# Dense block in fp32: rows normalised and turned from the tiles in which they were summed, one block later

## The chip, the cores and the metric

The kernel runs on one core of a Trainium2 chip. The metric is the device time of one launch in microseconds (us); less is better. Engines are named as the profile names them: PE (TensorE, matrix products), DVE (VectorE), ACT (ScalarE), POOL (GpSimd) and SP (SyncE, which here only issues DMAs).

## The reference

Two layers, each an attention block with 32 heads and then a dense block with a squared relu, all in fp32, on 2048 rows of 640 columns (the width F of the dense block is 1536). The normalisations have no weights.

```python
def _A_ref(x, wqkv, wo):                       # attention, 32 heads of 20
    q, k, v = split_heads(x @ wqkv)
    p = _softmax(einsum("bhqd,bhkd->bhqk", q, k) * (Dh ** -0.5))
    return merge_heads(einsum("bhqk,bhkd->bhqd", p, v)) @ wo
def _B_ref(x, w1, b1, w2, b2):                 # dense
    h = jnp.einsum("bsd,df->bsf", x, w1) + b1
    r = jnp.where(h > zero, h, zero)
    return jnp.einsum("bsf,fd->bsd", r * r, w2) + b2
for _ in range(2):
    x = x + _A_ref(_layernorm(x, axis=-1), A_wqkv, A_wo)
    x = x + _B_ref(_layernorm(x, axis=-1), B_w1, B_b1, B_w2, B_b2)
```

## The kernel before

Every fp32 operand of a product is split into a high and a low part, and three products of parts make one (`THREE`). The 2048 rows go in four blocks (`qb` 0 to 3) of 512, a block in four row tiles of 128 x 640. PSUM has eight banks, taken in turn.

A layer's dense block begins with the output projection, `add_heads(qb)`: for each row tile two chains of 15 matmuls (L361), half a row tile each, and a VectorE addition (L1355) that adds them to the tile of x; the finished tile is written to memory (`x_mid`, shown as `d_x<-x`). Then comes `mlp(fh, qb)`, for each half `fh` of the width F and each block: six "up" chains of 15 matmuls (L361) with relu and square on ScalarE (L1456, L1457, tiles `r`) and splits on VectorE (`upper` makes `ha`; `left_operands` makes three `hs` in seven instructions, L1438 to L1443 and L325), and then seven "low" products (L1482) whose banks VectorE adds to the rows (L1501; L1503 adds the bias). Half 0 leaves its sums in `d_half`, half 1 writes the next layer's input `x_e` (or the output).

An up chain needs the rows normalised and turned, tiles `xnT`, five of 128 x 512 for a block. Two generators make them, each step of which is run at a numbered place between the chains:

- `turn_out(d, xs)`: for each of four row tiles the statistics (L312, L313; POOL makes the reciprocal deviation at L315, L316), the normalisation in place (L320), a transpose of 32 x 32 squares into a tile `y` (L1389), and four stores of `y` into a buffer in memory, `d_t`, in pieces of 128 bytes.
- `turn_in(d, get)`: five loads xnT<-d_t, and for each a copy on ScalarE (L1405) and a subtraction on VectorE (L1406) that split it in two.

In the projection the places are the `side()` calls behind each half row (24 for the blocks behind the first); in an mlp they are one before it (-1), one behind each up chain, one behind the six, and one behind each low product. In half 1 the second use of a block's `xnT` comes from a copy in memory, `d_xn`.

Where the rows come from: block 0 is turned from the tiles in which `add_heads` summed it (`kept`). Blocks 1, 2 and 3 are read back from `x_mid` (`x<-d_x`), two tiles ahead: block 1 during the third and fourth block of the projection, block 2 in mlp(0,0), block 3 in mlp(0,1). In the first layer's half 1 the rows of block qb - 1 of the next layer's input are read back from `x_e` in mlp(1, qb). Block 3 of that input stays in tiles (`rows_3`) and is turned by PE (L476, in `turns`) at the hand-over, behind matmuls of the next layer's q, k, v (L399); `second()` yields the price by which those transposes are placed.

Each engine runs its instructions in the order written. All DMAs named here go through SP's queue in order, each waiting for the one eight places ahead of it; a tile of a pool is free for its next user when the last reader of the old contents is done, for `y` its stores. Row tiles, `y` and `r` share a pool of NX = 11 tiles of 2560 bytes a partition; xnT, hs, ha, weights and more share NSLOT = 42 tiles of 4096 bytes. An mlp also reads its own four rows (`row_tile(d_half if fh else x_mid, ...)`).

## Time and profile before

| | |
|---|---|
| median of 3 runs | 3516.32 us (3511.18 to 3517.25) |
| profiled execution | 3514.18 us, of which the span shown is 3512.4 us |
| granted PE clock, mean | 0.992 |
| busy, share of the span | PE 98%, DVE 81%, ACT 77%, POOL 23% |
| DMA | 533.20 MB, mean 152 GB/s; 179764 of 405510 packets under 512 bytes |
| dense block of layer 1 | 1342.5 to 1769.1 us of the span |
| dense block of layer 2 | 3095.4 to 3508.9 us |

All times in the profile count from the start of the span. "Waited for" names the last releaser of an instruction. PEclk is the granted clock of PE, 1.00 at full speed.

### The profile page before, as it was taken

What the parts mean: (1) busy time and instruction counts of PE and PEld (TensorE: products, weight loads), DVE (VectorE), ACT (ScalarE), POOL (GpSimd) and SP (SyncE); (2) the same over time, 40 slices, a digit from 0 to 9 for tenths busy, and PEclk for the clock granted to TensorE, in tenths of its full rate; (3) what the DMA queues carried; (4) which work ended last, traced back from release to release, by engine and by line L of the source; (5) the groups of instructions that cost most, each with busy time, mean ns of one, the idle gap of its engine ahead of it and who ended that gap; (6) DMA issues with size and microseconds to landing.
All of it is one profiled execution on the core that took longest, in us unless ns stands there. A gap on an engine that the chain in (4) does not pass through costs nothing.

```text
span 3512.4 us, 70196 instructions
## 1 busy us (share of the span) xinstructions
PE 3446.9 (98%) x26202; PEld 2158.6 (61%) x26202; DVE 2850.4 (81%) x5410; ACT 2705.2 (77%) x4362; POOL 800.5 (23%) x963
## 2 busy tenths in 40 slices
PE   9999999999999999899999999999999999998999
PEld 7897444444444447788889964444444444477898
DVE  8888999999999982656768889999999999726555
ACT  3778999999999992243337789999999999922433
POOL 6531445522112111100044201221221122111000
PEclk9999999999999999999999999999999999998999
DMA  9865555422211148957687652222232111488653
GB/s 311 280 239 170 182 159 180 149 74 77 61 51 46 43 121 256 282 209 253 175 280 264 204 161 80 69 77 66 68 83 58 52 43 43 129 264 265 213 224 109
DMA packets 405510, 533.20 MB, mean 152 GB/s; under 512 B 179764, under 2 KB 227380, under 8 KB 405168
## 3 DMA queue, kind: packets, MB, share of 16 engines
q1 hardware_dynamic: 404352, 526.35, 47.7%
q8 instruction: 206, 3.38, 0.4%
q10 hardware_dynamic: 816, 2.36, 0.2%
q14 instruction: 136, 1.11, 0.1%
HBM read 316.59 MB, written 211.98 MB: 150 GB/s over the span
## 4 chain that ended last, share of the span: by engine, by line
PE 90%; DVE 4%; DMA 3%; SPq 1%; ACT 1%; issue 1%; POOL 0%; DVEq 0%; POOLq 0%
PE banks L690 28%; PE banks L549 19%; PE banks L676 14%; PE banks L399 11%; PE banks L361 9%; PE banks L1482 7%; DMA x<-d_x 1%; SPq L76 1%; DVE bst L312 1%; DMA w<-d_w 1%; DVE x L320 0%; DVE y L1389 0%; ACT hs L324 0%; PE banks L1288 0%; DMA d_t<-y 0%
## 5 line engine op out<-in xcount | busy, mean ns | idle before, releaser
L561 DVE TENSOR_REDUCE mx<-banks 128x1 f32<-128x512 f32 x2096 | 1429.9, 686 | 136.9 <-PE banks L549 36.6
L549 PE MATMUL banks<-k,q 60*128 60x512 f32 (+1 forms) x4488 | 1310.3, 370 | 1.9 <-DVE v L445 1.9
L549 PEld LDWEIGHTS banks<-k,q 60*128 60x128 f32 x4488 | 714.7, 184 | 831.2 <-DVE mx L596 725.3
L684 ACT ACTIVATE e<-banks 128x512 f32<-128x512 f32 x1988 | 1194.1, 601 | 15.0 <-PE banks L676 2.2
L690 PE MATMUL banks<-e,vg 128*32 128x512 f32 x8192 | 1092.7, 605 | 1.5 <-ACT e L1295 1.5
L676 PE MATMUL banks<-q,k 62*128 62x512 f32 x3968 | 1074.3, 421 | 0.6 <-DVE mx L617 0.6
L686 ACT ACTIVATE e<-banks 128x1024 f32<-128x1024 f32 x990 | 1007.0, 1017 | 0.0
L596 DVE TENSOR_REDUCE mx<-banks 128x2 f32<-128x512 f32 x928 | 633.4, 682 | 3.3 <-PE banks L549 3.3
L676 PEld LDWEIGHTS banks<-q,k 62*128 62x128 f32 x3968 | 579.4, 184 | 53.8 <-ACT e L684 51.9
L617 DVE CUSTOM_DVE_ANT_0 rl<-banks,rl 128x512 f32<-128x512 f32 x536 | 350.2, 689 | 78.0 <-PE banks L549 57.2
L609 ACT ACTIVATE rl<-banks 128x512 f32<-128x512 f32 x538 | 295.7, 596 | 100.9 <-PE banks L549 80.2
L399 PE MATMUL banks<-xnT,wqk 64*128 64x512 f32 x2400 | 372.3, 393 | 0.9 <-DVE x L1501 0.6
L361 PE MATMUL banks<-xnT,w 128*128 128x512 f32 x1440 | 334.7, 393 | 11.0 <-DVE xnT L1406 8.1
L690 PEld LDWEIGHTS banks<-e,vg 128*32 128x32 f32 x8192 | 161.2, 108 | 260.7 <-issue 256.7
L399 PEld LDWEIGHTS banks<-xnT,wqk 64*128 64x128 f32 x2400 | 299.4, 186 | 25.6 <-issue 2.0
L361 PEld LDWEIGHTS banks<-xnT,w 128*128 128x128 f32 x1440 | 271.9, 190 | 69.6 <-DVE xnT L1406 10.1
L1482 PE MATMUL banks<-w,hs 128*128 128x320 f32 x1728 | 275.5, 319 | 20.4 <-DVE x L1501 13.5
L1482 PEld LDWEIGHTS banks<-w,hs 128*128 128x128 f32 x1728 | 266.2, 196 | 26.3 <-DVE x L1501 15.9
L1456 ACT ACTIVATE r<-banks,b_t 128x512 f32<-128x512 f32 x96 | 65.9, 687 | 261.1 <-PE banks L361 220.5
L339 POOL CAST mr<-nt 128x32 fp32r<-128x32 f32 x64 | 13.5, 212 | 1081.7 <-DVE nt L643 1081.7
L734 POOL TENSOR_TENSOR few<-few,minus_t 128x16 f32<-128x16 f32 x62 | 179.9, 2902 | 198.7 <-DMA few<-d_s 198.4
L399 PE MATMUL banks<-wv,xnT 64*128 64x320 f32 x1920 | 208.6, 307 | 0.8 <-ACT mark_t L401 0.8
(104 smaller groups left out, 2659.2 us busy)
## 6 DMA issues: line engine op xcount, KB each, us to landing
q<-d_qk SPq DMA_DIRECT2D x240, 240.0 KB
d_qk<-ev SPq DMA_DIRECT2D x80, 512.0 KB
k<-d_qk SPq DMA_DIRECT2D x152, 240.0 KB
w<-d_w SPq DMA_DIRECT2D x56, 480.0 KB
x<-d_x SPq DMA_DIRECT2D x84, 320.0 KB
d_qk<-ev SPq DMA_DIRECT2D x80, 256.0 KB
d_xn<-xnT SPq DMA_DIRECT2D x40, 512.0 KB
xnT<-d_xn SPq DMA_DIRECT2D x40, 512.0 KB
```

The costliest lines, as they stand in the source:

```text
L361: nc.tensor.matmul(dst, a, b, start=(n == 0), stop=(n == last))
L399: m = nc.tensor.matmul(ch["dst"][:, :width], *pair, start=first, stop=last)
L549: return nc.tensor.matmul(dst, q_t[t][b : b + 60, p, sub * P : (sub + 1) * P], k_t[t // NQB, c][b : b + 60, p, keys], start=True, stop=True,)
L561: nc.vector.tensor_reduce(maxima(t)[:, 2 * par + p, sub, c : c + 1], dst, axis=AX.X, op=ALU.max)
L596: r = nc.vector.tensor_reduce(maxima(t)[:, p : p + 3 : 2, sub, c if not half else column(t, p, sub)], bank.rearrange("q (r k) -> q r k", r=2),
L609: nc.scalar.activation(res, dst, AF.Relu)
L617: nc.vector.tensor_tensor_reduce(out=r, in0=dst, in1=r, scale=1.0, scalar=LEAST, op0=ALU.add, op1=ALU.max, accum_out=maxima(t)[:, 2 * par ...
L676: nc.tensor.matmul(dst, k_t[t // NQB, kt // 4][b : b + 62, p, (kt % 4) * P : (kt % 4 + 1) * P], q_t[t][b : b + 62, p, :], start=True, stop ...
L684: nc.scalar.activation(es[h], dst, AF.Exp, scale=SCALE)
L686: nc.scalar.activation(es[pair], banks[:, 1:3, :], AF.Exp, scale=SCALE)
L690: nc.tensor.matmul(acc[32 * h : 32 * h + 32, :], v_t[t // NQB, kt // 8][:, kt % 8, 32 * h : 32 * h + 32], es[h], start=(kt == 0), stop=(kt ...
L1482: nc.tensor.matmul(dst[:, :HALF], t[:, hx, c : c + P], w_2.piece(j, p, hw), start=start and p == 0 and (hx, hw) == THREE[0], stop=stop and ...
```

## The change

Every row tile that the projection sums is kept and turned during the block behind it: block 0 during qb = 1, block 1 during qb = 2, block 2 during qb = 3 and block 3 in mlp(0,0). In layer 1's half 1, the four row tiles that mlp(1, qb) finishes are kept (`rows`) and turned in mlp(1, qb + 1), their first statistics at place 18 of the mlp in which they were summed. No row is read back for turning, and `turn_out` loses its reads: 36 DMAs of 320 KB leave SP's queue (24 in layer 1, 12 in layer 2). By the order, all other counts stay (DVE 5412 instructions, ACT 4376, POOL 968, PE 22106).

`turn_in` of block 0 runs its steps at places 10, 14, 15, 17, 19, 21 of the projection (8, 12, 13, 16, 18, 20 before). The buffers `d_t` of the blocks are four in place of two in half 0. Rows 0 and 1 of the last block of layer 1 are normalised between its last low products, and `second()` yields 5.0 in place of 0.65. NX goes from 11 to 12, NSLOT from 42 to 41.

```diff
@@ -32,8 +32,8 @@
 LEAST = -3.0e38
 SCALE = DH ** -0.5
 NBLK = NG * NQB
-NSLOT = 42
-NX = 11
+NSLOT = 41
+NX = 12
 
 
 @with_exitstack
@@ -1355,17 +1355,11 @@
                 nc.vector.tensor_add(x[:, c], dst[:, :HALF], x[:, c])
                 side()
             dma(nc.sync, x_mid[(qb * 4 + i) * P : (qb * 4 + i + 1) * P, :], x)
-            if qb == 0:
-                kept.append(x)
+            kept.append(x)
+            x = None
 
     def turn_out(d, xs):
 
-        if callable(xs):
-            read, xs = xs, []
-            xs.extend(read(i) for i in range(2))
-        else:
-            read = None
-        yield
         y = None
 
         def store(i):
@@ -1387,8 +1381,7 @@
             normalise(nc.vector, xs[i], mvs[i])
             y = xtile("y")
             nc.vector.transpose(y, xs[i])
-            if read and i < 2:
-                xs.append(read(i + 2))
+            xs[i] = None
             yield
         store(3)
         xs.clear()
@@ -1416,7 +1409,7 @@
         nc.vector.tensor_scalar(y, x, mv[:, 0:1], mv[:, 1:2], op0=ALU.subtract, op1=ALU.mult)
         return y
 
-    def mlp(fh, qb, xnt, x_mid, x_dst, side, last):
+    def mlp(fh, qb, xnt, x_mid, x_dst, side, last, rows):
 
         xs, ops = [], {}
         w = QB // 2
@@ -1508,7 +1501,11 @@
                     dma(nc.sync, (x_dst if fh else d_half)[r0 : r0 + P, :], x)
                     if final and not last:
                         rows_3.append((x, stats(x) if j == 4 else None))
+                    elif fh and not last:
+                        rows.append(x)
                     xs[i] = None
+                if final and not last and (j, u) in ((5, 1), (6, 0)):
+                    rows_3[1 - u] = to_normal(*rows_3[1 - u])
                 x = None
                 side()
             if j == 0:
@@ -1522,12 +1519,10 @@
                 if not fh:
                     for n in (2 * j, 2 * j + 1):
                         w_2.load(1, n)
-        for i, (x, mv) in enumerate(rows_3[:]):
-            if i == 3:
-                rows_3[i] = x, stats(x)
-            else:
-                rows_3[i] = to_normal(x, mv or stats(x))
-        x = None
+        if final and not last:
+            for i in (2, 3):
+                rows_3[i] = rows_3[i][0], stats(rows_3[i][0])
+            rows_3[2] = to_normal(*rows_3[2])
 
     def layer(first, x_a, x_m, x_e, front_0, ahead):
         xs = []
@@ -1552,34 +1547,29 @@
         def rows_of(src, tb):
             return lambda i: row_tile(src, tb * 4 + i)
 
-        xnt, rows = [], []
-        plan = [[] for _ in range(24)]
-        outs = [turn_out(d_t[0], rows_of(x_m, 2))]
+        xnt = []
         loads = [
             [lambda s=s: w_1.load(s) for s in range(8)] + [lambda s=s: w_2.load(0, s) for s in range(3)],
             [lambda s=s: w_2.load(0, s) for s in range(3, 8)],
             [lambda s=s: w_2.load(0, s) for s in range(8, 12)],
             [],
         ]
-
+        plan = [[] for _ in range(24)]
+        in_0 = turn_in(d_t[0], lambda: xnt)
+        for i in (10, 14, 15, 17, 19, 21):
+            plan[i].append(lambda: next(in_0))
         for qb in range(NQB):
             if qb + 2 == NQB:
                 xnt.extend(new_rows())
+            rows = []
             add_heads(qb, x_a, x_m, xs, side, rows)
+            if qb + 1 < NQB:
+                gen = turn_out(d_t[qb], rows)
+                for i in (0, 1, 3, 5, 6, 7):
+                    plan[8 * qb + i].append(lambda gen=gen: next(gen))
             if qb == 0:
-                out_0 = turn_out(d_t[0], rows)
-                in_0 = turn_in(d_t[0], lambda: xnt)
-                out_1 = turn_out(d_t[1], rows_of(x_m, 1))
-                for gen, at in (
-                    (out_0, range(7)), (out_1, (13, 14, 15, 17, 19, 20)),
-                    (in_0, (8, 12, 13, 16, 18, 20)), (outs[0], (20,)),
-                ):
-                    for i in at:
-                        plan[i].append(lambda gen=gen: next(gen))
                 steps.extend([None] * (24 - len(steps)))
                 steps[:] = [(lambda n=n, f=f: [f and f()] + [g() for g in plan[n]]) for n, f in enumerate(steps)]
-            if qb == 1:
-                next(out_1)
             for f in loads[qb]:
                 f()
             if qb + 1 == NQB:
@@ -1587,6 +1577,8 @@
         w_o.drop()
         for s in range(12, w_2.n):
             w_2.load(0, s)
+        outs = [(turn_out(d_t[3], rows), (-1, -1, 0, 2, 4, 5))]
+        rows = None
         for fh, qb in ((fh, qb) for fh in range(2) for qb in range(NQB)):
             new = []
             plan = [[] for _ in range(22)]
@@ -1609,22 +1601,22 @@
                     dma(nc.sync, new[k], d_xn[qb, k])
 
             if not fh and qb + 1 < NQB:
-                put(turn_in(d_t[(qb + 1) % 2], to(new)), 6, 13, 14, 15, 16, 17)
+                put(turn_in(d_t[qb + 1], to(new)), 6, 13, 14, 15, 16, 17)
                 plan[20].append(lambda: [dma(nc.sync, d_xn[qb + 1, k], new[k]) for k in range(KD)])
             elif (fh, qb) != (1, NQB - 1):
                 plan[7].append(lambda: again((qb + 1) % NQB))
-            if not fh and qb + 2 < NQB:
-                put(outs.pop(0), -1, -1, 0, 2, 4, 5)
-            if not fh and qb + 3 < NQB:
-                outs.append(turn_out(d_t[(qb + 1) % 2], rows_of(x_m, qb + 3)))
-                put(outs[0], 17)
+            if outs:
+                put(*outs[0][:1], *outs.pop()[1])
+            rows = []
+            if ahead and fh and qb + 1 < NQB:
+                gen = turn_out(d_t[2 + qb], rows)
+                put(gen, 18)
+                outs.append((gen, (-1, 0, 2, 4, 5)))
             if (fh, qb) == (0, 0):
                 plan[4].append(lambda x=list(xnt): [dma(nc.sync, d_xn[0, k], x[k]) for k in range(KD)] and x.clear())
             if not fh and qb + 1 == NQB:
                 for n in range(7):
                     plan[(0, 0, 2, 4, 4, 4, 5)[n] + 1].append(lambda n=n: w_1.load(8 + n))
-            if ahead and fh and qb:
-                put(turn_out(d_t[1 + qb], rows_of(x_e, qb - 1)), -1, 0, 0, 2, 4, 6, 7)
             if ahead and fh and qb + 2 >= NQB:
                 for tb, at in enumerate((13, 6, 11)):
                     if (tb == 0) == (qb + 2 == NQB):
@@ -1636,7 +1628,8 @@
                     plan[11 + n].append(lambda n=n: w_qk.load(n))
             steps.extend((lambda p=p: [f() for f in p]) for p in plan)
             side()
-            mlp(fh, qb, xnt, x_m, x_e, side, not ahead)
+            mlp(fh, qb, xnt, x_m, x_e, side, not ahead, rows)
+            rows = None
             xnt = new
             all_steps()
         steps.clear()
@@ -1646,7 +1639,7 @@
 
 
         rows_3[3] = to_normal(*rows_3[3])
-        yield 0.65, turns(3, rows_3, ps_q, (1, 3))
+        yield 5.0, turns(3, rows_3, ps_q, (1, 3))
 
     def constants():
 
```

Three places as the order of instructions shows them, before and then after. Tiles carry a running number; lines of the changed kernel are six lower at the transpose (L1383 is L1389 of before) and seven lower behind it (L1494 is L1501).

SP's queue, layer 1, end of the projection and start of mlp(0,0). `d_x_111` is `x_mid`, `d_t_106` to `d_t_109` the buffers, `w` a weight tile. Before:

```order
698 L76 DMA d_t_107<-y_16189 32x20x32 x4
699 L76 DMA x_16214<-d_x_111 128x640
700 L76 DMA x_16216<-d_x_111 128x640
701 L76 DMA d_x_111<-x_15984 128x640
702 L76 DMA d_x_111<-x_16030 128x640
703 L76 DMA w_16268<-d_w_97 128x960
704 L76 DMA w_16270<-d_w_97 128x960
705 L76 DMA x_16289<-d_x_111 128x640
706 L76 DMA d_t_106<-y_16287 32x20x32 x4
707 L76 DMA x_16326<-d_x_111 128x640
708 L76 DMA x_16360<-d_x_111 128x640
709 L76 DMA x_16382<-d_x_111 128x640
```

After:

```order
694 L76 DMA d_t_108<-y_16167 32x20x32 x4
695 L76 DMA d_x_111<-x_15957 128x640
696 L76 DMA d_t_108<-y_16216 32x20x32 x4
697 L76 DMA d_x_111<-x_16011 128x640
698 L76 DMA d_t_108<-y_16265 32x20x32 x4
699 L76 DMA d_t_108<-y_16289 32x20x32 x4
700 L76 DMA d_x_111<-x_16060 128x640
701 L76 DMA w_16312<-d_w_97 128x960
702 L76 DMA w_16314<-d_w_97 128x960
703 L76 DMA d_t_109<-y_16331 32x20x32 x4
704 L76 DMA x_16400<-d_x_111 128x640
705 L76 DMA x_16422<-d_x_111 128x640
```

Of before, blocks 1 (`d_t_107`) and 2 (`d_t_106`) are being stored there, with reads `x<-d_x` between; two of these (16360, 16382) are mlp(0,0)'s own rows and stay. After, blocks 2 (`d_t_108`) and 3 (`d_t_109`) are being stored at this place, a block further on.

DVE in mlp(1,1) of layer 1, behind the split of the last `ha`, up to the first addition of a low product. In front of the rows of before stand, behind that split, the statistics L312 and L313 of the row 18210. Before:

```order
2101 L320 TENSOR_SCALAR x_18138<-x_18138,mv_18201 128x640
2102 L1389 STREAM_TRANSPOSE y_18281<-x_18138 128x640
2103 L1438 TENSOR_TENSOR s_18301<-r_18261,r_18298 128x256
2104 L1439 TENSOR_TENSOR s_18301<-s_18301,r_18261 128x256
2105 L325 TENSOR_TENSOR hs_18302<-r_18298,hs_18302 128x512
2106 L325 TENSOR_TENSOR hs_18303<-s_18301,hs_18303 128x512
2107 L1442 TENSOR_TENSOR s_18301<-r_18298,s_18301 128x256
2108 L1443 TENSOR_TENSOR s_18301<-r_18261 128x256
2109 L325 TENSOR_TENSOR hs_18304<-s_18301,hs_18304 128x512
2110 L320 TENSOR_SCALAR x_18210<-x_18210,mv_18274 128x640
2111 L1389 STREAM_TRANSPOSE y_18330<-x_18210 128x640
2112 L1501 TENSOR_TENSOR x_18172<-banks,x_18172 128x320
```

After, from the split on:

```order
2101 L325 TENSOR_TENSOR ha_18246<-r_18243,ha_18246 128x256
2102 L320 TENSOR_SCALAR x_17880<-x_17880,mv_18185 128x640
2103 L1383 STREAM_TRANSPOSE y_18256<-x_17880 128x640
2104 L1431 TENSOR_TENSOR s_18276<-r_18243,r_18273 128x256
2105 L1432 TENSOR_TENSOR s_18276<-s_18276,r_18243 128x256
2106 L325 TENSOR_TENSOR hs_18277<-r_18273,hs_18277 128x512
2107 L325 TENSOR_TENSOR hs_18278<-s_18276,hs_18278 128x512
2108 L1435 TENSOR_TENSOR s_18276<-r_18273,s_18276 128x256
2109 L1436 TENSOR_TENSOR s_18276<-r_18243 128x256
2110 L325 TENSOR_TENSOR hs_18279<-s_18276,hs_18279 128x512
2111 L1494 TENSOR_TENSOR x_18156<-banks,x_18156 128x320
```

The statistics of a row and one row's normalisation and transpose no longer stand between `ha` and the first addition (L1494 there); they come earlier in the mlp, and each row's steps one place sooner.

PE at the hand-over to layer 2: transposes L476 of the last block's rows and the q, k, v chains L399. Before:

```order
8611 L399 MATMUL banks<-xnT_18799,wqk_19184 128x512
8612 L399 MATMUL banks<-xnT_18799,wqk_19202 128x512 x2
8613 L399 MATMUL banks<-xnT_18799,wqk_19210 128x512
8614 L476 MATMUL banks<-ident,y_19330 128x128
8615 L476 MATMUL banks<-ident,y_19332 128x128
8616 L476 MATMUL banks<-ident,y_19341 128x128
8617 L476 MATMUL banks<-ident,y_19358 128x128
```

After:

```order
8641 L399 MATMUL banks<-xnT_18759,wqk_19176 128x512
8642 L399 MATMUL banks<-xnT_18759,wqk_19154 128x512
8643 L399 MATMUL banks<-xnT_18759,wqk_19176 128x512
8644 L476 MATMUL banks<-ident,y_19254 128x128
8645 L476 MATMUL banks<-ident,y_19269 128x128
8646 L476 MATMUL banks<-ident,y_19300 128x128
8647 L476 MATMUL banks<-ident,y_19310 128x128
```

The first L476 stands at number 8614 before and at 8644 after: 30 matmuls L399 have moved ahead of it.

## The prediction, made before the changed kernel ran

> **What bounds the kernel now.** I read the page first, then the stages of the two dense blocks as stretches, then who TensorE and VectorE wait for in them, then single waits in order of time.
>
> ```profile
> span 3512.4 us, 70196 instructions
> PE 3446.9 (98%) x26202; PEld 2158.6 (61%) x26202; DVE 2850.4 (81%) x5410; ACT 2705.2 (77%) x4362; POOL 800.5 (23%) x963
> ...
> PE banks L690 28%; PE banks L549 19%; PE banks L676 14%; PE banks L399 11%; PE banks L361 9%; PE banks L1482 7%; DMA x<-d_x 1%; SPq L76 1%; DVE bst L312 1%; DMA w<-d_w 1%; DVE x L320 0%; DVE y L1389 0%; ACT hs L324 0%; PE banks L1288 0%; DMA d_t<-y 0%
> ```
>
> TensorE (PE) carries the span: 65.5 us of 3512.4 are idle, and no change of order can win much more than those and what a lowered clock adds to its busy time. The chain that ended last holds the reads x<-d_x (1%, about 35 us), which is what the change removes. The stretches of the dense blocks, columns span, then PE, PEld, DVE, ACT, POOL busy, granted clock, DMA share and GB/s:
>
> ```profile
> 1342.50:1417.10 74.60, 72.07 (x486) 70.78 (x482) 30.65 (x61) 3.64 (x6) 5.87 (x12) 1.00 0.89 289
> 1417.10:1476.00 58.90, 45.95 (x217) 39.36 (x218) 39.94 (x83) 17.39 (x29) 5.78 (x12) 0.88 0.90 259
> 1476.00:1520.00 44.00, 40.40 (x218) 35.42 (x217) 30.12 (x64) 17.36 (x29) 3.85 (x8) 1.00 0.67 195
> 1520.00:1559.00 39.00, 39.00 (x218) 35.44 (x217) 21.51 (x44) 17.15 (x29) 0.00 (x0) 1.00 0.47 170
> ...
> 1636.70:1680.00 43.30, 40.42 (x217) 36.61 (x216) 30.34 (x62) 14.34 (x24) 3.81 (x8) 0.96 0.63 183
> 1680.00:1723.80 43.80, 40.93 (x218) 36.91 (x217) 31.89 (x65) 17.45 (x29) 3.92 (x8) 0.96 0.73 210
> 1723.80:1769.10 45.30, 41.26 (x217) 36.67 (x215) 35.57 (x77) 20.54 (x34) 5.98 (x12) 0.96 0.70 197
> ...
> 3095.40:3170.90 75.50, 73.21 (x486) 72.24 (x482) 31.55 (x63) 3.63 (x6) 6.57 (x14) 0.98 0.91 292
> 3170.90:3232.10 61.20, 48.08 (x218) 41.33 (x218) 39.05 (x81) 17.35 (x29) 5.08 (x11) 0.86 0.83 246
> 3232.10:3275.50 43.40, 41.50 (x218) 36.62 (x217) 30.19 (x63) 17.44 (x29) 3.85 (x8) 0.96 0.68 197
> ```
>
> In order: the output projection; mlp(0,0); mlp(0,1); mlp(0,2), which turns nothing and runs without a gap, so 39.0 us is what an mlp costs; then mlp(1,1), (1,2), (1,3); and layer 2's projection, mlp(0,0), mlp(0,1). Just those that turn rows (DVE over 30 us) are longer: by 19.9, 5.0, 4.3, 4.8, 6.3 in layer 1, and 22.2 and 4.4 in layer 2. All that this change can win lies there and at the hand-over to layer 2.
>
> ```profile
> PE banks L1482 <- DVE x L1501: 12.2, 6, 2.9
> ...
> PE banks L1482 <- ACT ha L324: 6.0, 2, 5.7
> ```
> ```profile
> DVE bst L312 <- DMA x<-d_x: 19.0, 7, 7.9
> ...
> DVE bst L312 <- DMA x<-d_x: 18.8, 5, 8.9
> ```
>
> PE's waits (layer 1, then layer 2) are on VectorE and ScalarE; VectorE in turn waits in order at bst (L312) for the rows that come back from memory, 19 us in each layer's dense block.
>
> **Clock.** A gap costs more than its length. The two stretches around the 2.87 us gap that starts at 1708.5, and one behind the 3.03 us gap of mlp(0,0):
>
> ```profile
> 1455.00:1460.00 5.00, 5.00 (x21) 5.00 (x22) 3.29 (x7) 3.50 (x7) 0.00 (x0) 0.58 0.86 248
> ...
> 1705.00:1710.00 5.00, 3.53 (x24) 3.11 (x22) 4.20 (x9) 1.24 (x2) 0.17 (x1) 1.00 1.05 343
> 1710.00:1715.00 5.00, 3.60 (x15) 3.60 (x16) 4.37 (x10) 0.00 (x0) 0.00 (x0) 0.68 0.70 118
> ```
>
> At 0.68 over 5 us the stretch loses 5 x 0.32 = 1.6 us of work; I call it a dip and price it at 1.7 (0.58 would be 2.1). The Trainium skill (TensorE: Matmul & The Clock Gate, "Why this matters for your kernels") wants idle gaps above about 3 us before the clock falls to half; here 2.87 sufficed. By that rule a removed gap would win its length alone, and my sum below would be about 14 us smaller.
>
> **Part 1, layer 1's second half (mlp(1,1) to (1,3)).** mlp(1,1), VectorE and then PE:
>
> ```profile
> 1659.40 0.88 DVE L312 BATCH_NORM_STATS2 bst<-x 128x6 f32<-128x320 f32 x2
> 1660.31 0.21 DVE L313 BATCH_NORM_AGGREGATE mv<-bst 128x2 f32<-128x12 f32 x1
> ...
> 1666.00 0.61 DVE L320 TENSOR_SCALAR x<-x,mv 128x640 f32<-128x640 f32 x1
> 1666.64 0.84 DVE L1389 STREAM_TRANSPOSE y<-x 128x640 f32<-128x640 f32 x1
> 1667.41 2.44 DVE L1501 TENSOR_TENSOR x<-banks,x 128x320 f32<-128x320 f32 x6
> ...
> 1667.91 4.36 PE L1482 MATMUL banks<-w,hs 128*128 128x320 f32 x19 [2.88 <-DVE x L1501]
> ```
>
> PE has filled its banks at 1665.0 and waits until L1501 empties one at 1667.9. Ahead of L1501 stand a row's statistics and another's normalisation and transpose, because rows read back could not start earlier. Afterwards the statistics of row 0 sit at the end of the mlp before, each row moves up one place, and these four items (0.88 + 0.21 = 1.1, to 1660.4 by the overlapping starts 1.05; and 1666.00 to 1667.41 = 1.4) leave the stretch: 2.5 of 2.88. Left: about 0.4 idle, too short for a dip by everything seen here. Gain (2.88 - 0.4) + 1.7 = 4.1 each, three times: 12.4, taken as 12. The other mlp parts of a row still fit: the first half's places cost VectorE time only while PE runs up chains. Bounds for the three: 2.2 if each ended at the 43.4 us of layer 2's mlp(0,1) (nearly this order on VectorE, but behind a late read), 15.4 if each ran in 39.0. The price of 4.1 is nearer to the second, since no read is waited for.
>
> **Part 2, hand-over.** PE, just behind the last mlp:
>
> ```profile
> 1769.63 3.71 PE L399 MATMUL banks<-xnT,wqk 64*128 64x512 f32 x30 [0.58 <-DVE x L1501]
> ...
> 1776.45 1.20 PE L476 MATMUL banks<-ident,y 128*128 128x128 f32 x5 [2.26 <-DVE y L1416]
> ```
>
> The yield of 5.0 puts another 30 matmuls ahead of L476, 3.7 us by the first row, against a wait of 2.26; two of the four normalisations are also earlier. Those matmuls have to be done anyway, so the place costs nothing. Gain 2.26 + one dip 1.7 = 4.0; bounds 0 (another row late) and 4.
>
> **Part 3, mlp(0,1).** It no longer turns anything: its 44.0 and 43.4 become 39.0. Its chain began at a read:
>
> ```profile
> 1437.17 5.76 DMA x<-d_x
> ...
> 1481.60 5.29 DMA x<-d_x
> ```
>
> Gain 5.0 in layer 1 and 4.4 in layer 2; what could be late next is xnT for mlp(0,2), whose stores now end a whole mlp earlier, so nothing. Bounds: 4 to 5 a layer.
>
> **Part 4, projection and mlp(0,0).** Gone is the read above at 1437.17 and those like it. PE there:
>
> ```profile
> 1409.83 7.24 PE L361 MATMUL banks<-wo,ot 128*128 128x320 f32 x45 [2.38 <-DVE x L1355]
> ...
> 1424.55 1.22 PE L361 MATMUL banks<-xnT,w 128*128 128x512 f32 x3 [2.89 <-DVE xnT L1406]
> 1427.32 19.88 PE L361 MATMUL banks<-xnT,w 128*128 128x512 f32 x77 [1.55 <-DVE xnT L1406]
> 1450.66 1.75 PE L1482 MATMUL banks<-w,ha 128*128 128x320 f32 x9 [3.03 <-ACT ha L324]
> ...
> 1454.89 4.98 PE L1482 MATMUL banks<-w,hs 128*128 128x320 f32 x19 [1.22 <-DVE hs L325]
> ```
>
> The gaps of 2.89 and 1.55 wait for xnT(0), loaded from the stores of block 0: they stay. Those of 2.38 (VectorE stuck at the split of xnT with L1355 behind; a chain later now) and of 3.03 and 1.22 (behind the read of 5.76) can go, with their two dips: 2.38 + 3.03 + 1.22 + 3.4 = 10.0, and up to 13 with the small ones behind. Against that, the DMA queue is the other resource at its end in this place (share 0.89 and 0.90 above). SP issues in order:
>
> ```profile
> 1442.74 1.48 SPq L76 DMA_DIRECT2D x<-d_x  x3
> ...
> 1453.98 8.58 SPq L76 DMA_DIRECT2D d_t<-y  x8
> ...
> 1462.65 2.38 SPq L76 DMA_DIRECT2D xnT<-d_t  x5
> 1469.96 1.64 SPq L76 DMA_DIRECT2D d_half<-x  x2
> ```
>
> Up to 1476 ten reads leave (blocks 1 and 2, two of block 3), at 0.49 each about 5 us; the 16 stores of block 3 come in from mlp(0,1), at 8.58/8 = 1.07 each 17 us where the queue is full. Net 12 us more. Behind them stand the loads of xnT for mlp(0,1): they were issued by 1465.0, with nothing on the queue until 1469.96, and mlp(0,1) begins at 1476.0. The hole of 4.9 and some 4 us of lead before the splits take 9 of the 12 (an estimate), so I give 3 back: 10.0 - 3 = 7 in layer 1. In layer 2 the same gap on ha is 5.7 instead of 3.03, so 2.7 more: 10. Bounds: 13 and 16 if nothing comes back; -2 and 1 if all 12 us do.
>
> **Costs taken as nothing.** A slot less (41), a row tile more and three buffers d_t in place of two: no row shows a wait by which to price the slot; the nearest is a row tile's, 18.0 us of ScalarE under a store, which PE did not feel:
>
> ```profile
>   ACT r L1456: 18.0, 1
> ```
>
> So 0, with PE's own 2.26 above as the far end. Instruction counts of PE, VectorE, ScalarE and POOL stay; 36 reads of 320 KB leave SP. The stores, the loads xnT<-d_t and the reads that each mlp makes of its own rows stay.
>
> **Sum.** Layer 1: 12 + 4 + 5.0 + 7 = 28. Layer 2, which has no hand-over: 4.4 + 10 = 14.4. Together 42.4. The profiled execution took 3514.2, so 3471.8; the median, 3516.3, is 2.1 above it, and as the result is a median I say 3474.
>
> **Rivals.** (a) The queue takes the place of the reads: part 4 is worth nothing, because rows wait for tiles that the stores hold where they waited for reads. For it: DMA share 0.9, and the 18.0 us wait. Against: PE's gaps there follow reads in the chain. 25.4 are left: 3491. (b) The relief is larger: part 4 gives its 13 + 16, no stage keeps its 0.4: 12 more there, and part 1 its 15.4, 3.4 more: 3458.5. (c) The lowered clock is not the gaps' doing and stays: eight dips less (three in the second half, one at the hand-over, two in each mlp(0,0)), 13.6 us: 3488. Against it stands the clock, 1.00 ahead of such a gap and 0.68 behind it. The rule of the Trainium skill named above comes to the same, for gaps of this length. (d) The reads were hidden anyway and other work is late at the same places: no change, 3516. The gaps of mlp(1,1) speak against it, being VectorE's own work. (e) Slower: r (L1456) in mlp(0,0) gets its tile from the row tiles, which rows now keep for a block longer, until 16 late stores have gone. PE has the six up chains as cover (19.88 us for 77 of their 90 matmuls), less the first one, about 17 us: a longer wait turns into idle PE, one for one. Parts 1 to 3 give 25.4, so it needs 17 + 13 = 30 us of wait in each layer to eat them; with 36 the kernel ends at about 3528. The 18.0 seen is near the first bound and far from the second.
>
> **Chances.** The forecast 0.55; (a) 0.20; (b) 0.08; (c) 0.05; (d) 0.04; (e) 0.08. Faster by over 0.2% (7 us, about what a measurement of this kernel tells from none): 0.55 + 0.20 + 0.08 + 0.05 = 0.88; same 0.04; slower 0.08. The range runs from just below (b), 3455, past (a) to 3502, where (a) has lost a stage of part 1 and the hand-over and a little more; outside are (d), (e) and some of (b), under 0.2.
>
> **What would show it.** No x<-d_x wait at bst; mlp(0,1) at 39 us with 44 VectorE instructions; mlp(1,1) to (1,3) at 39.5 with L1482's wait for L1501 below 0.5 and clock 1.00; no gap ahead of L476; projection and mlp(0,0) together near 126.5 us (133.5 now) in layer 1. I am wrong if r or y waits for d_t<-y there for longer than 17 us, if the 2.9 us gaps come back with another releaser, or if the dips stay.

## The result, and the profile after

| | before | after |
|---|---|---|
| median of 3 runs | 3516.32 us | 3495.11 us (3491.35 to 3496.46) |
| profiled execution, span | 3514.18, 3512.4 us | 3491.35, 3489.6 us |

The ratio is 0.9941, 95% interval 0.9919 to 0.9964: 21.2 us faster, where 42.4 were forecast and the range went to 3502. Measured a second time, with 5 runs, the changed kernel took 3495.42 against 3512.15, ratio 0.9952 (0.9939 to 0.9964).

The head of the page of the changed kernel:

```profile
span 3489.6 us, 70164 instructions
...
PE 3439.0 (99%) x26202; PEld 2152.2 (62%) x26202; DVE 2850.0 (82%) x5410; ACT 2704.5 (78%) x4362; POOL 799.2 (23%) x963
```

Its stages as stretches (columns as before: span, then PE, PEld, DVE, ACT, POOL busy, clock, DMA share, GB/s). In order: projection, mlp(0,0), mlp(0,1); mlp(1,1), (1,2), (1,3); layer 2's projection, mlp(0,0), mlp(0,1).

```profile
1341.10:1412.50 71.40, 71.40 (x487) 70.92 (x484) 38.40 (x77) 3.69 (x6) 8.43 (x18) 1.00 0.88 285
1412.50:1476.10 63.60, 49.46 (x218) 41.69 (x217) 41.12 (x87) 17.50 (x29) 6.81 (x15) 0.84 0.91 240
1476.10:1515.00 38.90, 38.90 (x217) 35.37 (x216) 21.42 (x44) 17.15 (x29) 0.00 (x0) 1.00 0.45 160
1631.60:1670.50 38.90, 38.90 (x218) 35.36 (x217) 30.04 (x63) 14.45 (x24) 3.74 (x9) 1.00 0.60 170
1670.50:1711.30 40.80, 39.47 (x218) 35.42 (x217) 30.80 (x63) 17.55 (x29) 3.68 (x8) 1.00 0.67 194
1711.30:1752.90 41.60, 39.19 (x217) 35.14 (x215) 35.91 (x77) 20.66 (x34) 6.25 (x12) 1.00 0.69 203
3079.40:3150.90 71.50, 71.50 (x487) 71.02 (x484) 38.19 (x77) 3.69 (x6) 8.21 (x18) 1.00 0.89 282
3150.90:3213.80 62.90, 48.44 (x218) 40.81 (x217) 41.28 (x88) 17.49 (x29) 6.97 (x15) 0.84 0.90 235
3213.80:3252.70 38.90, 38.90 (x218) 35.37 (x217) 21.42 (x43) 17.15 (x29) 0.00 (x0) 1.00 0.47 170
```

Both projections now run without a gap, mlp(0,1) and mlp(1,1) are at their 38.9, and (1,2) and (1,3) are close. But mlp(0,0) is longer, with a clock of 0.84: 63.6 us. Projection and mlp(0,0) together went from 133.5 to 135.0 us in layer 1 and from 136.7 to 134.4 in layer 2. Nearly all of part 4 of the prediction, 17 us, is missing there. PE in mlp(0,0) of layer 1:

```profile
1417.75 1.65 PE L361 MATMUL banks<-xnT,w 128*128 128x512 f32 x3 [2.85 <-DVE xnT L1399]
1421.53 19.17 PE L361 MATMUL banks<-xnT,w 128*128 128x512 f32 x77 [2.13 <-DVE xnT L1399]
...
1461.84 2.90 PE L1475 MATMUL banks<-w,hs 128*128 128x320 f32 x18 [1.20 <-DVE x L1494]
1467.93 1.92 PE L1475 MATMUL banks<-w,hs 128*128 128x320 f32 x9 [3.19 <-DVE x L1494]
1471.01 5.05 PE L1475 MATMUL banks<-w,hs 128*128 128x320 f32 x18 [1.16 <-DVE x L1494]
```

The gaps at the start stayed, as forecast. The gap on `ha` fell from 3.03 to 0.73, but in the last fifteen microseconds three others came up, with a dip behind them: those 18 matmuls from 1471.01 take 5.05 us where 18 from 1461.84 took 2.90. All three wait for L1494 (L1501 of before). The longest waits of VectorE that lie in front of them, out of 1413 to 1477:

```profile
DVE x L1494 <- DMA x<-d_x: 5.2, 1, 5.2
DVE xnT L1399 <- ACT xnT L1398: 4.6, 1, 4.6
```

Neither is a row to be turned. The first is one of the four rows that mlp(0,0) reads for its own sum, the second the split of xnT for mlp(0,1), with L1494 queued behind it. SP's queue shows why they are late:

```profile
1440.79 5.20 SPq L76 DMA_DIRECT2D d_t<-y  x4
1446.03 1.40 SPq L76 DMA_DIRECT2D x<-d_x  x2
1447.53 2.72 SPq L76 DMA_DIRECT2D d_t<-y  x4
1450.30 0.55 SPq L76 DMA_DIRECT2D x<-d_x  x1
1450.95 4.56 SPq L76 DMA_DIRECT2D d_xn<-xnT  x5
1455.62 1.13 SPq L76 DMA_DIRECT2D x<-d_x  x1
1456.84 6.37 SPq L76 DMA_DIRECT2D d_t<-y  x8
1463.32 2.37 SPq L76 DMA_DIRECT2D xnT<-d_t  x5
```

Without a break the queue issues stores of block 3, reads of rows, the five copies d_xn<-xnT of block 0 and more stores. The fourth row is issued at 1455.6, behind the copies, and its addition starts at 1461.3; the loads of xnT are issued from 1463.3. So the reads that were waited for went, and theory 1 is that the stores of a block that came in their place made other reads late. Theory 2: the work of turning block 3 keeps VectorE itself. Theory 3: `y` and `r` wait for row tiles that stores hold.

### The profile page after: what moved, and what is told of

Its sections match the earlier page's. It is cut to its first block, busy times and chain, and to the rows that moved or that the text cites. A ratio compares the mean times of both kernels' runs of the same rounds, so it can differ in the third digit from the quotient of the medians.

```text
span 3489.6 us, 70164 instructions
## 1 busy us (share of the span) xinstructions
PE 3439.0 (99%) x26202; PEld 2152.2 (62%) x26202; DVE 2850.0 (82%) x5410; ACT 2704.5 (78%) x4362; POOL 799.2 (23%) x963
## 5 line engine op out<-in xcount | busy, mean ns | idle before, releaser
L561 DVE TENSOR_REDUCE mx<-banks 128x1 f32<-128x512 f32 x2096 | 1430.1, 686 | 135.4 <-PE banks L549 34.4
L399 PE MATMUL banks<-xnT,wqk 64*128 64x512 f32 x2400 | 372.3, 393 | 1.8 <-DVE x L1494 1.1
L399 PEld LDWEIGHTS banks<-xnT,wqk 64*128 64x128 f32 x2400 | 296.8, 186 | 29.8 <-issue 2.0
L399 PE MATMUL banks<-wv,xnT 64*128 64x320 f32 x1920 | 208.8, 307 | 0.8 <-ACT mark_t L401 0.8
```

Of the source, the lines that this page charges most:

```text
L399: m = nc.tensor.matmul(ch["dst"][:, :width], *pair, start=first, stop=last)
L561: nc.vector.tensor_reduce(maxima(t)[:, 2 * par + p, sub, c : c + 1], dst, axis=AX.X, op=ALU.max)
```

## The experiments

The runs were measured in three groups, each with the kernel before beside it: 3512.15 us in the first (the changed kernel again, the second half alone, the copies moved, block 3 later), 3514.58 in the second (the first half alone, 14 row tiles, and the next two combinations) and 3511.9 in the last four. Between groups the ratio to before is what to compare. Stage lengths are read from the start of the projection's first matmul to the end of mlp(0,0)'s last in the profile of each, one profile a kernel. Where a few us are too few for the times to tell, the stages tell.

**The base, and the halves apart.** First the changed kernel again, unedited:

> The changed kernel once more, timed beside the others of this call. It serves as the base for them: about 0.994 of before (3495 against 3516). Whatever the cause of the missing 21 us, the projection and mlp(0,0) of layer 1 should again take about 135.0 us together and of layer 2 134.4 (133.5 and 136.7 before). If the 3.4 us by which layer 2's attention was longer in the first profile (matmuls 15200 to 24000 fell back from -19.6 to -16.0 us) belong to the change, they show again; if they are of that execution, they do not.

3495.42 us; 135.4 and 134.6 us in the two layers, as expected. Layer 2's attention, PE's matmuls 16000 to 23900, took 1010.2 us before, 1013.5 in the first profile of the changed kernel, 1012.5 in this one, and 1010.3 and 1009.6 in the first two kernels of the part on the queue, which hold the change as well. So the 3 us did show again, but the change does not bring them by itself; in all the kernels of this study the stretch, whose work is the same, took 1009.4 to 1013.5, and why is open.

The change in layer 1's second half and the hand-over, put on the kernel before (with `rows`, `rows_3` and the yield as the change has them):

```diff
-NSLOT = 42
-NX = 11
+NSLOT = 41
+NX = 12
...
-                put(turn_out(d_t[1 + qb], rows_of(x_e, qb - 1)), -1, 0, 0, 2, 4, 6, 7)
+            if ahead and fh and qb + 1 < NQB:
+                gen = turn_kept(d_t[2 + qb], rows)
+                put(gen, 18)
+                kept_outs.append((gen, (-1, 0, 2, 4, 5)))
```

> The kernel before with the change in layer 1's second half and hand-over alone (rows kept in mlp(1,0) to (1,3), yield 5.0, 12 row tiles, 41 slots); projection and half 0 as before. By the profile of the change, mlp(1,1) to (1,3) give 11.1 us and the hand-over 3.5, less the 2.4 and 0.6 us that came up in front of it (counted in the 11.1): 14 to 15 us, ratio 0.996 (3501). If the two halves interact through pools or queue, it is not 0.996; if the hand-over gives nothing at all, 11 us, 3505.

3503.69 us, ratio 0.9971 (0.996 to 0.9983), between the two values. In its profile mlp(1,1) to (1,3) take 38.9, 40.4 and 43.0 us (43.4, 43.8 and 45.2 before), projection and mlp(0,0) of the two layers 134.0 and 136.9.

And the other half, the changed kernel with those parts taken back:

```diff
-            if ahead and fh and qb + 1 < NQB:
-                gen = turn_out(d_t[2 + qb], rows)
-                put(gen, 18)
-                outs.append((gen, (-1, 0, 2, 4, 5)))
+            if ahead and fh and qb:
+                put(turn_read(d_t[1 + qb], rows_of(x_e, qb - 1)), -1, 0, 0, 2, 4, 6, 7)
...
-        yield 5.0, turns(3, rows_3, ps_q, (1, 3))
+        yield 0.65, turns(3, rows_3, ps_q, (1, 3))
```

> The changed kernel with layer 1's second half and the hand-over as before (rows read back, yield 0.65): the change in the projection and half 0 alone, 12 row tiles and 41 slots. mlp(0,1) gives 9.5 us in the two layers, projection and mlp(0,0) nothing (+1.5 and -2.3 by the first profile): 9 to 11 us less than before, ratio 0.997 (3502). Together with the second half alone (0.9971, 8.5 us) it should make the whole (0.995); by the stages of the profiles the second half is worth 13, and what is missing is scatter of the executions.

3507.15 us, ratio 0.9976 (0.9966 to 0.9986). Projection and mlp(0,0) take 134.5 and 137.4, mlp(0,1) 38.9 and 39.4: all that the first half's change gives is mlp(0,1). 8.5 and 7.4 us (each against before in its group) make 16 of the 17 us that the whole gave in the second measurement: within the intervals the halves add up.

**The queue.**

```diff
-  plan[4].append(lambda x=list(xnt): [dma(nc.sync, d_xn[0, k], x[k]) for k in range(KD)] and x.clear())
+  plan[8].append(lambda x=list(xnt): [dma(nc.sync, d_xn[0, k], x[k]) for k in range(KD)] and x.clear())
```

> The changed kernel, but the five copies d_xn<-xnT of block 0 (512 KB each) are issued behind the loads of xnT for mlp(0,1) and not ahead of mlp(0,0)'s fourth row. Theory 1 (queue): in mlp(0,0) VectorE's additions wait for that row (5.2 us) and behind it for the split of xnT (4.6 us), because both stand in SP's queue behind block 3's stores and these copies, which take 4.6 us of it. Then the wait for the row falls below 1 us, that for xnT below 1 us, the gaps 1.20, 3.19 and 1.16 on PE and the low clock from 1469 go, and each layer gains 5 to 8 us: ratio near 0.990 (3482). Theory 2 (VectorE): the work of turning block 3 in mlp(0,0) itself makes the additions late; then nothing changes within 0.1%, 3495. Theory 3 (row tiles): r and y wait for tiles that stores hold; also no change, since the stores keep their places.

3480.24 us, ratio 0.9907 (0.9894 to 0.9921): 15 us less than the changed kernel by five copies moved, with the same work on VectorE. VectorE's waits in its mlp(0,0):

```profile
DVE xnT L1399 <- ACT xnT L1398: 4.9, 3, 4.1
DVE x L320 <- DMA d_x<-x: 3.8, 1, 3.8
```

The wait for the fourth row is gone, that for xnT is not: its loads still stand behind block 3's stores. The second line (2.5 us in the changed kernel) is a wait that the change brought: a kept row is normalised in place, and first its own write to `x_mid` has to have read it. Projection and mlp(0,0): 130.2 and 127.7 us, 5.2 and 6.9 less than the base. The second part of the expectation (xnT below 1 us) did not come true. Theory 2 is out as the whole cause.

```diff
-            if outs:
+            if outs and (fh, qb) != (0, 0):
                 put(*outs[0][:1], *outs.pop()[1])
```

> The changed kernel, but block 3 is turned in mlp(0,1) (from its kept tiles) in place of mlp(0,0). Theory 1 (queue): the 16 stores leave the full stretch, so mlp(0,0) loses the gaps behind the fourth row and xnT (5.5 us and a dip of 3.4 a layer), and mlp(0,1) goes as mlp(1,1) does after the change, with no more than 0.5 us over 38.9: 7 to 9 us a layer, 3479. Theory 2 (VectorE): as much VectorE work moves to mlp(0,1) and costs there what it costs now: gain of mlp(0,0) given back, within 2 us of 3495. Theory 3 (row tiles): four tiles stay taken through mlp(0,0), so r waits longer: slower than 3495.

3471.39 us, ratio 0.9881 (0.9866 to 0.9896): 24 us less than the base, more than expected. Its projection, mlp(0,0) and mlp(0,1) in layer 1:

```profile
1342.10:1414.70 72.60, 71.74 (x487) 71.00 (x484) 37.79 (x76) 3.63 (x6) 7.82 (x18) 1.00 0.86 273
1414.70:1467.30 52.60, 43.08 (x218) 37.99 (x217) 32.61 (x69) 17.59 (x29) 3.89 (x7) 0.90 0.90 257
1467.30:1506.10 38.80, 38.80 (x217) 35.28 (x216) 30.17 (x63) 17.56 (x29) 3.78 (x8) 1.00 0.70 204
```

mlp(0,0) loses 11.0 us against the first profile of the changed kernel, and the projection in front of it takes 1.2 more; together the two take 125.2 us, and 126.8 in layer 2, 10.2 and 7.8 less than the base. mlp(0,1), which now turns block 3 with 30 us of VectorE, runs without a gap: there, with a DMA share of 0.70, the same VectorE work costs nothing, and the four kept tiles do no harm. This edit moves block 3's stores and its VectorE work together, so what is due to each in mlp(0,0) is not separated; the edit before moved the order of the queue alone.

```diff
-NSLOT = 41
-NX = 12
+NSLOT = 40
+NX = 14
```

> The changed kernel with 14 row tiles and 40 slots in place of 12 and 41. Theory 3 (row tiles): the waits of y (L1383) and r (L1449) for stores d_t<-y, 7.9 and 1.0 us in layer 1's projection and mlp(0,0), go, and with them a part of the gaps: 3 to 6 us a layer, 3485 to 3489. Theory 1 (queue): y and r wait less, but the fourth row and xnT come no sooner: 3495 within 2 us, ratio 0.995.

3489.7 us, ratio 0.9933 (0.9919 to 0.9947) against 0.9952 (0.9939 to 0.9964) of the base: about what theory 3 expected of the total. But projection and mlp(0,0) take 135.2 and 134.8 us, as in the base, and VectorE's longest waits in mlp(0,0) are the old two (no wait of y is left there, and 1.6 us in the projection):

```profile
DVE x L1494 <- DMA x<-d_x: 5.5, 1, 5.5
DVE xnT L1399 <- ACT xnT L1398: 4.7, 1, 4.7
```

Theory 3 falls for this stage. Where the rest of the total comes from is open, and the two intervals overlap; in the profile, the time from mlp(1,3) to layer 2's projection, where profiles scatter, is 2.3 us shorter than in the base.

The first two edits of this part together:

> The two earlier edits together: block 3 turned in mlp(0,1) and block 0's copies d_xn<-xnT issued behind the loads of xnT. In the run with block 3 alone moved, L1494 still waited once in mlp(0,0) (3.6 us in layer 1, 4.4 in layer 2), where the mlp's fourth row is issued behind these copies. Theory 1 (queue): that wait goes with its dip, about 5 us a layer: ratio 0.985 to 0.986 (3462 against 3512). If the wait was on VectorE's order and not on that row, nothing is added: 0.988.

3459.55 us, ratio 0.9842 (0.9829 to 0.9856). Projection and mlp(0,0) take 119.7 and 119.4 us: moving the copies gives 5.5 and 7.4 a layer here as well, so the last wait of L1494 was the fourth row.

**The start of mlp(0,0).** There PE still waited twice for xnT, in the kernel with both edits:

```profile
1418.57 1.65 PE L361 MATMUL banks<-xnT,w 128*128 128x512 f32 x3 [3.10 <-DVE xnT L1399]
1422.35 20.58 PE L361 MATMUL banks<-xnT,w 128*128 128x512 f32 x77 [2.13 <-DVE xnT L1399]
```

On the changed kernel, with the copies behind as well:

```diff
-NSLOT = 41
-NX = 12
+NSLOT = 40
+NX = 14
...
                 gen = turn_out(d_t[qb], rows)
+                held.append((qb, gen))
+            if qb < 2:
                 for i in (0, 1, 3, 5, 6, 7):
                     plan[8 * qb + i].append(lambda gen=gen: next(gen))
...
-        outs = [(turn_out(d_t[3], rows), (-1, -1, 0, 2, 4, 5))]
+        outs = [(turn_out(d_t[3], rows), (-1, -1, 0, 2, 4, 5)), (held[2][1], (-1, -1, 0, 2, 4, 5))]
...
-                put(*outs[0][:1], *outs.pop()[1])
+                gen, at = outs.pop()
+                put(gen, *at)
```

> As the run with both edits, but now block 2 is turned in mlp(0,0) and block 3 in mlp(0,1), both from kept tiles, so that nothing but xnT's splits stands between the additions of the projection's last block (14 row tiles, 40 slots to hold them). It asks what holds the start of mlp(0,0), where PE waits 2 to 4 and then 2 to 3 us for the splits of xnT (L1399) in every kernel so far, with two dips: about 8 us a layer. Theory A (VectorE's order): block 2's statistics, transposes and waits for y stand between the splits; then these waits fall below 1 us: 10 to 16 us less in the two layers, ratio near 0.982, unless the 16 stores of block 2 cost mlp(0,0) as block 3's did. Theory B (queue): the loads of xnT land late because SP's queue is full; their place in the queue is the same, so the waits stay and the ratio is 0.986 or worse.

3456.11 us, ratio 0.9831 (0.9818 to 0.9845), by the ratio the fastest kernel of the study, 59 us or 1.7% below the kernel before. PE at the change from projection to mlp(0,0), and the longest gap behind it:

```profile
1404.71 9.11 PE L361 MATMUL banks<-wo,ot 128*128 128x320 f32 x61
1413.66 20.71 PE L361 MATMUL banks<-xnT,w 128*128 128x512 f32 x90
...
1442.11 1.31 PE L1475 MATMUL banks<-w,ha 128*128 128x320 f32 x6 [2.46 <-ACT ha L324]
```

All 90 matmuls of the up chains run in one piece, although the loads of xnT stand where they did: theory A. ScalarE's copies of the loaded tiles end at 1411.3 here and at 1410.2 in the kernel with both edits, so the data came no sooner; but the last split begins at 1415.9 in place of 1421.6. The wait had been VectorE's order, since block 2's steps stood between the splits (1.7 us of them a transpose that waited for stores). Of the 10 to 16 us expected only 1.6 and 2.2 a layer are left as gain (118.1 and 117.2 us against 119.7 and 119.4), because block 2's stores now make mlp(0,0) wait in turn, the 2.46 above: ScalarE's relu waits for a row tile that they hold.

```profile
1440.27 0.69 ACT L1449 ACTIVATE r<-banks,b_t 128x512 f32<-128x512 f32 x1 [2.19 <-DMA d_t<-y]
```

**Reads or copies?** The last kernel turns blocks 2 and 3 in the mlps in which the kernel before turned them, without the reads. Two runs complete a square: the last kernel with the copies at place 4 again, and the kernel before with them at place 8. The square is not a clean one, since the kernels with kept rows also have 14 row tiles, block 1 turned some places sooner and the change in the second half; so its stages are compared too.

> Blocks 2 and 3 turned in mlp(0,0) and mlp(0,1) from kept tiles, copies d_xn<-xnT in their old place ahead of mlp(0,0)'s fourth row: the kernel before's places of work with the reads alone taken away in half 0 (14 row tiles, 40 slots). Theory 1 (queue): the fourth row stands behind the copies again, 4 to 6 us a layer come back: 3465, ratio 0.986. If what made the difference was the splits of xnT alone, 3457, ratio 0.983.

> The kernel before (rows read back) with block 0's five copies d_xn<-xnT behind the loads of xnT, and nothing else. It has the blocks in the places of the run with blocks 2 and 3 later, so the two differ by the reads of rows and by the second half. Theory 1 (queue): the copies stood ahead of the last row for turning and of stores in mlp(0,0), so some of the 7 to 8 us a layer that the edit gave on the changed kernel comes here as well, but VectorE still waits for the row reads ahead of it (5.2 and 7.9 us in layer 1): 2 to 8 us in all, ratio 0.998. Rival: the reads were never the cost, the copies were; then it gives all 15 us and more: ratio 0.995 or below.

The copies at place 4 and at place 8 give 3511.9 and 3515.14 us (ratio 1.001, 1.0001 to 1.0019) with rows read, and 3470.4 (0.9882) and 3456.11 (0.9831, in the second group) with rows kept. So the edit alone gives nothing, a little loss rather: projection and mlp(0,0) take 134.6 and 136.2 us, about the 133.5 and 136.7 of before. VectorE waits for reads of rows as ever, one line for 1413 to 1525 (18.3 us before):

```profile
DVE bst L312 <- DMA x<-d_x: 22.2, 6, 8.5
```

With rows kept, projection and mlp(0,0) take 123.5 and 124.7 us with the copies ahead and 118.1 and 117.2 with them behind: they cost 5.4 and 7.5 a layer (beside the 3470.4, two near twins of the last kernel, below, took 3455.0 and 3457.55). In layer 1, VectorE in the kernel with the copies ahead, and the longest gap of PE there:

```profile
1452.19 0.89 DVE L1494 TENSOR_TENSOR x<-banks,x 128x320 f32<-128x320 f32 x2 [3.09 <-DMA x<-d_x]
1457.89 0.69 DVE L1399 TENSOR_TENSOR xnT<-xnT 128x512 fp32r<-128x512 f32 x1 [4.81 <-ACT xnT L1398]
...
1459.04 2.73 PE L1475 MATMUL banks<-w,hs 128*128 128x320 f32 x9 [3.40 <-DVE x L1494]
```

Both the fourth row and the loads of xnT for mlp(0,1) stand behind the copies, and the longer wait is that for xnT: the loads are issued at 1454.2 and not at 1448.0 as in the last kernel, and PE's gap ends with the addition behind their first split. Behind the fourth row PE waited 0.37 us. So moving the copies helps by both, here mostly by the loads of xnT, in the kernels above by the row.

Expected were 3465 and 2 to 8 us of gain; the first came out as 3470.4, the second missed its sign.

**The hand-over, and the next layer's loads.** Both on the kernel with blocks 2 and 3 later and the copies behind.

```diff
-        yield 5.0, turns(3, rows_3, ps_q, (1, 3))
+        yield 0.65, turns(3, rows_3, ps_q, (1, 3))
```

> The run with blocks 2 and 3 later and the copies behind, but with the yield 0.65 at the hand-over: L476 stands 30 matmuls sooner, right behind the normalisation of the last rows. By the trace of before its wait was 2.26 us with a dip of 1.7 behind it; two of the four rows are now normalised sooner, so the last row's statistics and normalisation remain: a wait of about 2 us and a dip, matmuls 13152 to 13400 take 34 to 34.5 us in place of 31.2: 3 us more, 3459, which the times hardly tell but the trace does. If the gain at the hand-over came from the normalisations and not from the yield, 31.2 stays.

3455.0 us, and matmuls 13152 to 13400 take 31.22 us, as with 5.0 (31.20; 34.49 before). PE there:

```profile
1745.83 0.55 PE L476 MATMUL banks<-ident,y 128*128 128x128 f32 x3
1746.71 0.76 PE L476 MATMUL banks<-ident,y 128*128 128x128 f32 x5 [0.33 <-DVE y L1409]
```

The expectation was wrong: without the 30 matmuls ahead, the earlier normalisations leave 0.33 us of the 2.26 us wait, so the yield of 5.0 is worth no more than that 0.33 beside them. Whether it would have done alone was not run. The stretch scatters with what lies in front of it: other kernels with 5.0 took 30.6 to 32.7 us.

```diff
-                for tb, at in enumerate((13, 6, 11)):
+                for tb, at in enumerate((9, 6, 11)):
...
-                        d = 3 if tb == 0 else 5
+                        d = 7 if tb == 0 else 5
```

> The run with blocks 2 and 3 later and the copies behind, with the loads xnT<-d_t of the next layer's block 0 issued at place 9 of mlp(1,2) in place of 13, their splits where they were. In mlp(1,2) VectorE waits 2.5 us for the first of them, with L1494 behind it and 1.5 us of PE. If the load is late because it is issued late, that wait goes: 1.5 us, up to 3.2 with a dip, 3453 to 3455. If the queue or the slots are full there, nothing changes: 3456.

3457.55 us, no change in time. VectorE's wait in mlp(1,2) for the first load fell from 2.5 to 1.9 us and the stage from 41.2 to 40.6. But the edit did not bring the loads forward. SP's queue, with the edit:

```profile
1672.58 9.03 SPq L76 DMA_DIRECT2D d_t<-y  x8
1681.71 2.61 SPq L76 DMA_DIRECT2D xnT<-d_xn  x5
1684.41 2.96 SPq L76 DMA_DIRECT2D xnT<-d_t  x5
```

The loads stand behind eight stores and five reads of copies and are issued 28.4 us after the stage's first matmul, 28.2 without the edit. That fits the second half of the expectation (the queue is full there), and whether loads that are issued sooner would help stays open.

## Why the prediction was wrong

- **The stages that bound** were read rightly: but for some 2 us of attention, all of the change lies in the stretches named, and the ones without turning stayed at 38.9.
- **Part 1** (second half): 12 forecast. 132.4 us became 121.3, so 11.1. mlp(1,1) has no gap. In (1,2) and (1,3) gaps of 1.05 and 2.41 us are left that the forecast did not have: L1494 stands behind splits of the next layer's xnT, in (1,3) also behind statistics of the last block's rows, with VectorE busy 4.93 and 5.00 of 5 us around the gap (rows in the last section).
- **Part 2** (hand-over): 4.0 forecast, 3.3 measured (34.49 to 31.20). The size was near, but the cause that the sentence put first was not needed: with the yield back at 0.65 the normalisations do it.
- **Part 3** (mlp(0,1)): 9.4 forecast, 9.6 measured (44.0 and 43.4 became 38.9).
- **Part 4** (projection and mlp(0,0)): 17 forecast, 0.8 measured (layer 1 lost 1.5, layer 2 won 2.3). This is the step that failed, and in it the sentence by which "the hole of 4.9 and some 4 us of lead" take 9 of the 12 us of added stores, "so I give 3 back". The hole was behind the loads of xnT, and the work that came in stands ahead of them and of the fourth row. In an ordered queue a hole behind does not help who stands in front of it: VectorE waited 5.2 us for that row and 4.6 for the split of xnT. Against the gross gain of the forecast, 10.0 and 12.7 us, the cost put at 3 a layer came to 11.5 and 10.4. With blocks 2 and 3 left in the mlps of before (copies at place 4), so that no stores move into this stretch, it did gain 10.0 and 12.0. That the sizes meet so well is in part luck: there the gaps at the start went but for 0.41 us, which the forecast had left standing, and one of 3.40 for xnT came up, which it did not have. The price of 12 us, with which the two layers were put at -2 and +1 (measured -1.5 and +2.3), is not the stores' alone either: five copies moved, with all 16 stores in place, brought 5.2 and 6.9 back. The gaps at the start, taken as fixed by the stores of block 0, were mostly not the queue's: with VectorE's order changed they went.
- **Rival (a)**, "the queue takes the place of the reads", 3491, was the case; measured 3495. Its mechanism was half right: no turned row waited for a tile to any cost (14 tiles changed nothing in the stage), but the mlp's own row and the next xnT waited behind stores. The prediction's own sign of being wrong came with it: a gap of 3.19 us with another releaser, L1494. **Rival (e)**, ScalarE's r waiting for row tiles, did show in layer 1's mlp(0,0): 1.0 us for stores and 14.4 for the transpose that frees a kept row. That is less than the 17 us of cover; with 14 tiles both are gone and the stage is as long. **Rival (c)** is out in its simple form: the clock in mlp(1,1) to (1,3) is 1.00, where it was 0.96 with the gaps; but it also is with the gap of 2.41 us that is left, so that a gap need not bring a dip (last section). **Rival (b)**'s 3458 was reached only by the kernels that turn two blocks later, with the copies behind.
- The sum by the stages of the two profiles: 11.1 + 3.3 + 9.6 + 0.8 = 24.8; the spans differ by 22.8, the rest being attention (1.4 us shorter in front of layer 1's dense block, 3.3 longer in layer 2). One sum of the prediction itself is off: by the rule of the Trainium skill that it quotes, the dips behind the gaps of 3.03 and 5.7 us would still go with their gaps, so the sum would shrink by six dips, about 10 us, and not by all eight, 14.

## What to carry to other kernels

Taking a read out of a full, ordered DMA queue pays only what the next instruction in that queue allows: price what comes in its place by who stands behind it, not by the free time at its end. Work that is kept on chip need not be done at once; here the tiles pay most when their stores stay where the queue has room (DMA share 0.70), with a few row tiles more to hold them. And look for bulk copies that nobody waits for soon: moving five of them behind an awaited row and the awaited loads of xnT was worth 12 to 15 us here, but nothing while VectorE still waited for rows read back.

## What the runs showed of the hardware

A gap's length alone does not decide whether the clock falls. In the kernel before, gaps of 2.87 and 2.26 us were followed by a clock of 0.66 to 0.68 over 5 us. In the changed kernel, two stretches around a gap of 2.41 us before 1750.0; in the fastest kernel, around one of 2.78 before 1735.2; and in the kernel with block 3 later and the copies behind, around one of 1.83 before 1694.3:

```profile
1745.00:1750.00 5.00, 2.60 (x18) 2.33 (x16) 4.93 (x13) 3.42 (x6) 1.94 (x4) 1.00 1.04 408
1750.00:1755.00 5.00, 3.85 (x26) 3.45 (x28) 5.00 (x11) 0.26 (x1) 0.22 (x1) 1.00 1.03 409
```
```profile
1730.00:1735.00 5.00, 2.40 (x17) 2.13 (x15) 4.93 (x13) 3.09 (x5) 1.76 (x4) 1.00 1.03 399
1735.00:1740.00 5.00, 3.67 (x24) 3.31 (x26) 5.00 (x11) 0.62 (x1) 0.41 (x1) 1.00 1.03 409
```
```profile
1690.00:1695.00 5.00, 3.17 (x21) 2.91 (x20) 2.17 (x4) 1.79 (x3) 0.00 (x0) 0.97 1.02 359
1695.00:1700.00 5.00, 5.00 (x22) 4.75 (x22) 4.93 (x12) 1.23 (x2) 1.08 (x2) 0.69 0.22 84
```

The two longer gaps left it at 1.00, the shorter one cost a dip. The plainest pair is the last kernel of the experiments, which has a gap of 2.71 us in front of the same matmuls (before 1735.8) as the fastest one its 2.78. Around and behind it the clock fell:

```profile
1735.00:1740.00 5.00, 4.03 (x18) 3.63 (x18) 4.52 (x10) 1.55 (x3) 0.91 (x2) 0.72 1.03 410
1740.00:1745.00 5.00, 4.61 (x26) 3.66 (x28) 4.06 (x10) 0.00 (x0) 1.81 (x4) 0.60 0.48 189
```

The Trainium skill (TensorE: Matmul & The Clock Gate, "What's actually happening") says that the activity is judged in windows of about 3.4 us that run freely; that would let like gaps end differently. But it has the clock fall after a whole idle window, and the gaps of 1.83 to 2.87 us that cost a dip here are shorter than one, so in that the traces do not agree with it. No run here shows where the windows lie. For a forecast it means that a dip of 1.7 us behind a gap of 2 to 3 us is a chance and not a price.
